# One weight load of a fused attention and mixture-of-experts kernel, issued by ScalarE instead of the sync engine

## The chip, the core and the metric

The kernel runs on one core of one Trainium2 chip. The metric is the device time of one execution in microseconds (us). Before the change it is 284.03 us, the median of three runs that lie between 283.61 and 284.60 us.

The core has five engines with an instruction stream each: PE (TensorE, matrix products), DVE (VectorE), ACT (ScalarE), POOL (GpSimd) and SP (SyncE, which here only issues transfers). PEld is PE's loading of weights. Sixteen DMA engines move data between HBM and the core's memory. A transfer is issued by an instruction on an engine's stream and goes into that engine's queue: q1 in the profile is SP's queue, q10 is ScalarE's.

## The reference

An attention with a decaying state runs over 768 steps for each of 4 batches and 8 heads of width 48; its output, 3072 rows of 384, goes through a mixture of 4 experts with weights of 384 x 1024 and 1024 x 384.

```
for t in range(S):
    cur = einsum('bhd,bhe->bhde', u * k[t], v[t])
    y[t] = einsum('bhd,bhde->bhe', r[t], state + cur)
    state = w * state + einsum('bhd,bhe->bhde', k[t], v[t])
x = y, laid out as (B*S) x (H*D)
p = domain_probs / (domain_probs.sum(-1) + 1e-9)
for e in range(E):
    out += p[:, e] * (relu(x @ w1[e]) @ w2[e])
```

## The kernel before, in words

The attention is done in 24 chunks of 128 rows; chunk ci belongs to batch ci modulo 4, so the first four chunks are the first of the four batches. For a chunk the kernel loads r, k and v (tiles `RKin` and `Vt`, 192 KB each, line 270), multiplies r and k by powers of w into `RK_sb` (line 429), transposes them on PE (line 498) and copies them out to `RKT` (lines 79 and 81), multiplies them to `At_all` (line 546), masks that into `AtM` on DVE (line 560), and multiplies by v to `Y_ps` (line 593). Beside it POOL forms r*k into `ruk` (line 446) and times u (line 454; line 451 on DVE for chunk 0), DVE sums it into `dcoef` (line 467) and POOL makes `dv` from it (line 472). The result is transposed to `xTe` (line 645). Groups of four chunks then go through the experts: the first layer is `hT_ps` (line 751, 757), its relu is on ACT (line 766, 768), the second layer is `out_ps` (line 787). Later groups use a scheme with sums and differences of halves (`M_ps`, line 966).

The weights come as float32 in three pieces for each expert and layer, `PIECES = ((0, 3), (3, 6), (6, 8))` in blocks of 128 columns: 576, 576 and 384 KB. They land in one of four staging slots of the tile `stg` and are cast to bf16 into `w_sb` (line 79 on ACT, 81 on DVE, 83 on POOL). The middle piece of w1 of expert 0 is `("wst", 1, 0, 1)`; its cast is the first of ACT's casts of weights.

The order of every engine's instructions is written out by hand: `PLAN` is a string that names each job and its engine, and the kernel emits the jobs in that order. `load_w` makes one load job; its `run` takes the first slot from `st_free`, and the cast gives it back. SP's stream begins with k of chunk 0, v of 1, r of 1, r of 0, k of 1, r of 2, v of 0, r of 3, k of 2, k of 3, and then the middle piece and the last piece of w1 of expert 0, v of 2, the first piece, and v of 3. ACT's stream begins with a table load and three small loads of w and u (lines 93, 95 and 102) before its first job, the logarithm of w (line 345), from which PE makes `w_ps` (line 349) and ACT the powers `W_ps` (line 358).

Transfers take eight semaphores (`DMAHW0` to `DMAHW7`) in turn, in program order and over both queues. A transfer is issued only when the one that had its semaphore before, eight transfers earlier, has landed.

`spin` (line 246) puts matrix products on PE that nobody reads: seven before the first real one, and a written number before some jobs.

Of the kernel before, what the change touches and what calls it, by code (L numbers as in the profile page):

```python
# [18 lines left out]
def kernel(  # L19
# [12 lines left out]
    nc = tc.nc  # L32
# [9 lines left out]
    Dm = moe_w1.shape[1]  # L42
    F = moe_w1.shape[2]
    NDB = Dm // 128
# [19 lines left out]
    NST = 4  # L64
    NSTG = 8
    stg = weights.tile([128, NSTG, 3 * Dm], F32)
    stg_f = stg.rearrange("p a b -> p (a b)")
    stg_b = stg_f.bitcast(BF16)
    early = hAll.rearrange("p a s c -> p (a s c)").bitcast(F32)[:, 3 * NFB * SUB * 64:]
    w1_v = moe_w1.rearrange("e (db p) f -> e p db f", p=128)  # L70
# [3 lines left out]
    PIECES = ((0, 3), (3, 6), (6, 8))  # L74
# [162 lines left out]
    tl = {}  # L237
# [14 lines left out]
    def load_job(name, nbytes_us, run, takes=(), needs=()):  # L252
        q_rank[0] += 1
        job(name, {"S": 0.5}, run, needs, q_rank[0], takes, (), nbytes_us)
# [17 lines left out]

    at_of = {}
    touched = set()
    st_free = list(range(NST))

    def st_at(i):
        return 3072 + i * 3 * Dm

    def load_w(m, e, i):  # L280
        a, bb = PIECES[i]

        def run():
            tl["wst", m, e, i] = st_free.pop(0)
            t = stg_f[:, st_at(tl["wst", m, e, i]):][:, 0:(bb - a) * Dm]
            if m == 1:
                nc.sync.dma_start(t.rearrange("p (d f) -> p d f", d=NDB),
                                  w1_v[e][:, :, a * 128:bb * 128])
            else:
                nc.sync.dma_start(t.rearrange("p (f d) -> p f d", d=Dm),  # L290
                                  w2_v[e][:, a:bb, :])
        nd = 24 if m == 1 else 8 * (bb - a)
        us = 0.555 * (bb - a)
        if (m, e) not in touched:
            us += 0.37 if touched else 0.68
            touched.add((m, e))
        load_job(("wst", m, e, i), (us, nd), run,
                 (("wst", m, e, i),))
# [24 lines left out]
    def cast(m, e, i, rank):  # L323
        a, bb = PIECES[i]
        n = bb - a

        def run(eng):
            st_free.append(tl["wst", m, e, i])
            t = stg_f[:, st_at(tl["wst", m, e, i]):][:, 0:3 * Dm]
            if m == 1:  # L330
                copy_on(eng, w1_sb[:, e, :, a * 128:bb * 128],
                        t[:, 0:n * Dm].rearrange("p (d f) -> p d f", d=NDB))
            else:
                copy_on(eng, w2_sb[:, e, a:bb, :].rearrange("p f d -> p (f d)"), t[:, 0:n * Dm])
        on = {"A": 0.36 * n, "V": (0.43 if m == 1 else 0.23) * n}
        if e == 0:
            on = {"A": 0.36 * n}
            if m == 2:
                on["P"] = 0.36 * n
        job(("cast", m, e, i), on, run, [("wst", m, e, i)], rank, (),  # L340
            (("wst", m, e, i),))
# [995 lines left out]
```

## Time and profile before

| | |
|---|---|
| time, median of three runs | 284.03 us |
| time of the profiled execution | 283.63 us |
| its span, first to last instruction | 281.8 us |
| PE busy | 274.6 us (97%) |
| DVE, ACT, POOL busy | 189.1, 183.5, 111.1 us |
| granted clock of TensorE, mean | 1.000 of full speed |
| moved by DMA | 43.22 MB |

The profiled execution has 1.83 us outside its span. A row of a timeline gives the start of a group of instructions in us from the span's start, its length, engine, line, operation, tiles written and read, count, and in brackets how long the engine stood idle before it and what ended that. For a DMA issue (SPq, ACTq) the length is that of the issuing instruction, not of the transfer. Rows of the stages give busy us of each engine, the granted clock, the share of the 16 DMA engines in use (packets can overlap, so it can pass 1) and GB/s.

### The profile page before, as it was taken

How to read it: one execution, taken by the hardware profiler on the slowest of the kernel's cores; microseconds unless marked ns; L12 is line 12 of the kernel's file. 1: busy time of each engine (PE TensorE's matmuls, PEld its weight loads, DVE VectorE, ACT ScalarE, POOL GpSimd, SP SyncE). 2: the span in 40 equal slices, each digit the busy share in tenths (PEclk: the TensorE clock that was granted, in tenths of full speed). 3: DMA queues.
4: the chain of work that ended last, by engine and by line, in shares of the span. 5: the costliest groups of instructions: out<-in, count | busy, mean ns of one | idle time of the engine just before them, and what ended most of it. 6: DMA issues, size and time to landing. Idle time of an engine off the chain costs nothing.

```text
span 281.8 us, 6864 instructions
## 1 busy us (share of the span) xinstructions
PE 274.6 (97%) x2741; PEld 197.1 (70%) x2762; DVE 189.1 (67%) x334; ACT 183.5 (65%) x348; POOL 111.1 (39%) x134
## 2 busy tenths in 40 slices
PE   7899999999999999999999999999999999999995
PEld 2568567676665445899445899445899544899895
DVE  5964878998779646777537787355888706776071
ACT  5586756798852889744788752789754788521840
POOL 1985243875566565326862406476012000000000
PEclk9999999999999999999999999999999999999999
DMA  7999999899998897585994376993775500110202
GB/s 150 240 320 330 282 230 270 224 228 284 269 198 171 162 192 191 88 173 110 203 184 97 88 111 122 169 254 22 151 124 96 140 28 2 32 26 2 84 2 84
DMA packets 133491, 43.22 MB, mean 153 GB/s; under 512 B 121658, under 2 KB 133436, under 8 KB 133460
## 3 DMA queue, kind: packets, MB, share of 16 engines
q1 hardware_dynamic: 133300, 42.74, 70.1%
q8 instruction: 21, 0.34, 0.5%
q14 instruction: 10, 0.08, 0.1%
q10 hardware_dynamic: 160, 0.05, 0.1%
HBM read 26.79 MB, written 4.72 MB: 112 GB/s over the span
## 4 chain that ended last, share of the span: by engine, by line
PE 93%; DVE 2%; DMA 1%; ACT 1%; issue 1%; SPq 1%; POOL 0%; POOLq 0%
PE hT_ps L757 34%; PE M_ps L966 28%; PE out_ps L787 7%; PE hT_ps L1174 4%; PE hT_ps L1208 4%; PE out_ps L1191 4%; PE hT_ps L751 2%; PE At_all L546 2%; PE Y_ps L593 2%; DMA RKin<-in_r_dram 1%; PE St_ps L662 1%; PE Y_ps L586 1%; PE At_all L1123 1%; PE M_two L1123 1%; PE spin_ps L246 1%; DVE AtM L560 1%
## 5 line engine op out<-in xcount | busy, mean ns | idle before, releaser
L768 ACT ACTIVATE hAll<-hT_ps 128x512 bf16<-128x512 f32 x152 | 86.4, 597 | 25.4 <-PE hT_ps L757 22.7
L757 PE MATMUL hT_ps<-stg,w_sb 128*128 128x512 bf16 x370 | 85.6, 379 | 0.6
L757 PEld LDWEIGHTS <-w_sb 128*128 128x128 bf16 x456 | 42.5, 98 | 45.6
L966 PEld LDWEIGHTS <-hAll 128*128 128x128 bf16 x800 | 65.7, 98 | 1.1
L622 ACT ACTIVATE stg<-dv,p_nat 128x384 bf16<-128x384 f32 x72 | 41.3, 611 | 10.6 <-DMA stg<-stg 5.3
L446 POOL TENSOR_TENSOR ruk<-RKin 128x384 f32<-128x384 f32 x24 | 26.6, 1114 | 29.5 <-DMA RKin<-in_r_dram 17.9
L472 POOL TENSOR_TENSOR dv<-Vt,dcoef 128x384 f32<-128x384 f32 x24 | 21.5, 898 | 40.8 <-DVE dcoef L467 27.4
L966 PE MATMUL M_ps<-w_sb,hAll 128*128 128x192 bf16 x400 | 36.9, 246 | 0.0
L1000 ACT COPY o_sb<-M_ps 128x192 f32<-128x192 f32 x35 | 10.9, 316 | 38.2 <-PE M_ps L966 37.9
L681 POOL TENSOR_TENSOR S<-Tn,wC 64x192 bf16<-64x192 f32 x32 | 22.8, 712 | 23.9 <-DVE Tn L671 21.5
L928 DVE TENSOR_TENSOR stg<-hAll 128x1024 bf16<-128x1024 bf16 (+1 forms) x15 | 12.5, 836 | 25.5 <-ACT hAll L768 15.4
L454 POOL TENSOR_TENSOR ruk<-ruk,U_sd 128x384 f32<-128x384 f32 x23 | 24.7, 1076 | 1.0
L928 DVE TENSOR_TENSOR hAll<-hAll 128x1024 bf16<-128x1024 bf16 (+1 forms) x30 | 23.8, 803 | 0.6 <-PE M_ps L966 0.5
L787 PE MATMUL out_ps<-w_sb,hAll 128*128 128x384 bf16 x128 | 22.8, 326 | 0.0
L966 PE MATMUL M_ps<-o_sb,hAll 128*128 128x192 bf16 x200 | 20.3, 246 | 0.0
L966 PE MATMUL M_ps<-w_mix,hAll 128*128 128x192 bf16 x200 | 20.1, 246 | 0.0
L434 DVE TENSOR_TENSOR RK_sb<-RKin,W_both 128x768 bf16<-128x768 f32 x16 | 18.3, 1141 | 1.8 <-DMA RKin<-in_k_dram 1.8
L757 PE MATMUL hT_ps<-xTe,w_sb 128*128 128x512 bf16 x65 | 17.8, 379 | 0.4
L787 PEld LDWEIGHTS <-hAll 128*128 128x128 bf16 x128 | 12.0, 98 | 7.4
L608 DVE TENSOR_TENSOR dv<-Y_ps,dv 128x384 f32<-128x384 f32 x18 | 9.9, 551 | 8.3 <-PE Y_ps L593 6.9
L563 DVE TENSOR_TENSOR AtM<-At_all,mask 128x1024 bf16<-128x1024 f32 x8 | 9.8, 1219 | 8.4 <-PE At_all L546 7.9
L1002 DVE TENSOR_TENSOR o_sb<-o_sb,M_ps 128x192 f32<-128x192 f32 x25 | 8.5, 350 | 9.6 <-PE M_ps L966 3.3
(123 smaller groups left out, 392.8 us busy)
## 6 DMA issues: line engine op xcount, KB each, us to landing
stg<-in_moe_w_dram SPq DMA_DIRECT2D x16, 576.0 KB, 7.1
RKin<-in_k_dram SPq DMA_DIRECT2D x24, 192.0 KB, 4.0
Vt<-in_v_dram SPq DMA_DIRECT2D x24, 192.0 KB, 3.5
RKin<-in_r_dram SPq DMA_DIRECT2D x24, 192.0 KB, 4.2
out_dram<-o_sb SPq DMA_DIRECT2D x23, 192.0 KB, 2.3
stg<-in_moe_w_dram SPq DMA_DIRECT2D x8, 384.0 KB, 5.8
stg<-stg SPq DMA_TRANSPOSE x36, 2.8
RKT<-RK_sb SPq DMA_TRANSPOSE x16, 3.9
```

The lines of the kernel that those rows point to most:

```text
L434: job(("scale", ci, 0), {"V": SCALE_US}, lambda: nc.vector.tensor_mul(RK[:, :, :, 0:D], tl["in", ci], W_both), [("Rt", ci), ("Kt", ci), (" ...
L446: nc.gpsimd.tensor_mul(tl["ruk", ci], tl["Rt", ci], tl["Kt", ci])
L454: nc.gpsimd.tensor_mul(tl["ruk", ci], tl["ruk", ci], U_sd)
L472: nc.gpsimd.tensor_mul(tl["dv", ci], tl["Vt", ci], tl["dcoef", ci].to_broadcast((128, H, D)))
L622: nc.scalar.mul(o, tl["Ysb", ci], p_nat[:, e, n_p:n_p + 1])
L681: nc.gpsimd.tensor_mul(S_new[pr, :, cl], Tn2[pr, tn_at[ci], :, cl], wC[pr, :, None].to_broadcast((P2, NP, D)))
L757: nc.tensor.matmul(ps[:, 0:n, :].rearrange("p a b -> p (a b)"), w1_sb[:, e, db, fb * 128:(fb + 1) * 128], xTe[:, x0 + db, s0:s0 + n, :].re ...
L768: nc.scalar.activation(hTs[:, fb, s0:s0 + n, :], ps[:, 0:n, :], AF.Relu)
L787: nc.tensor.matmul(ps, relu_tile(e, sc)[:, fb, s, :], w2_sb[:, e, fb, :], start=(fb == 0), stop=(fb == NFB - 1))
L928: nc.vector.tensor_tensor(o, x, y, op=op)
L966: nc.tensor.matmul(tl["P", sc, q, m], st, moving(m, hf, (n + 4) % 8), start=(opens and n == 0), stop=(hf == 1 and n == 7), skip_group_chec ...
L1174: nc.tensor.matmul(ps[:, f, :], w1_sb[:, e, db, (a + f) * 128:(a + f + 1) * 128], get_xTe(1)[:, db, s, :], start=(f == 0 and db == 0), sto ...
```

## The change

The middle piece of w1 of expert 0 gets the fourth staging slot for itself. Its load is issued on ScalarE's queue in the preamble, right behind the three small loads and ahead of the logarithm, and waits for nothing. Its place in SP's stream, behind k of chunk 3, is empty now. The free list begins with three slots; the cast gives the fourth back to it as before.

```
-    st_free = list(range(NST))
+    st_free = list(range(NST - 1))

     def st_at(i):
         return 3072 + i * 3 * Dm

+    nc.scalar.dma_start(stg_f[:, st_at(NST - 1):][:, 0:3 * Dm].rearrange("p (d f) -> p d f", d=NDB),
+                        w1_v[0][:, :, PIECES[1][0] * 128:PIECES[1][1] * 128])
+
     def load_w(m, e, i):
         a, bb = PIECES[i]

         def run():
-            tl["wst", m, e, i] = st_free.pop(0)
+            tl["wst", m, e, i] = NST - 1 if (m, e, i) == (1, 0, 1) else st_free.pop(0)
             t = stg_f[:, st_at(tl["wst", m, e, i]):][:, 0:(bb - a) * Dm]
+            if (m, e, i) == (1, 0, 1):
+                return
             if m == 1:
                 nc.sync.dma_start(t.rearrange("p (d f) -> p d f", d=NDB),
                                   w1_v[e][:, :, a * 128:bb * 128])
```

On ACT the start of the stream was this (`hAll` holds the rows of w and u at this time):

```order
L93 DMA hAll_72<-in_w_dram 1x384 [waits DVE_49]
L95 DMA hAll_72<-in_u_dram 1x384 [waits DVE_49]
L102 DMA hAll_72<-in_w_dram 4x2x48 [waits DVE_49]
L345 ACTIVATE hAll_72<-hAll_72 1x384 [waits DMAHW2_49]
L79 CAST Vb_149<-Vt_135 128x384 [waits DMAHW1_49]
```

and it is now this:

```order
L93 DMA hAll_72<-in_w_dram 1x384 [waits DVE_49]
L95 DMA hAll_72<-in_u_dram 1x384 [waits DVE_49]
L102 DMA hAll_72<-in_w_dram 4x2x48 [waits DVE_49]
L280 DMA stg_73<-in_moe_w1_dram 128x3x384
L350 ACTIVATE hAll_72<-hAll_72 1x384 [waits DMAHW2_49]
L79 CAST Vb_150<-Vt_136 128x384 [waits DMAHW1_49]
```

One load is added ahead of the logarithm; every later instruction keeps its place, and lines behind the change are five higher.

On SP the stream from the fourth load on was this (`RKin_133`, `137`, `147` and `162` hold r and k of chunks 0 to 3, `Vt_135`, `151` and `226` v of chunks 1, 0 and 2):

```order
L270 DMA RKin_133<-in_r_dram 128x8x48
L270 DMA RKin_137<-in_k_dram 128x8x48
L270 DMA RKin_147<-in_r_dram 128x8x48 [waits DMAHW0_49]
L270 DMA Vt_151<-in_v_dram 128x8x48 [waits DMAHW1_49]
L270 DMA RKin_162<-in_r_dram 128x8x48 [waits DMAHW2_49]
L270 DMA RKin_147<-in_k_dram 128x8x48 [waits DMAHW3_49]
L270 DMA RKin_162<-in_k_dram 128x8x48 [waits DMAHW4_49]
L287 DMA stg_73<-in_moe_w1_dram 128x3x384 [waits DMAHW5_49]
L287 DMA stg_73<-in_moe_w1_dram 128x3x256 [waits DMAHW6_49]
L270 DMA Vt_226<-in_v_dram 128x8x48 [waits DMAHW7_49]
```

and it is now this (the numbers of these tiles are one higher, up to `163`):

```order
L270 DMA RKin_134<-in_r_dram 128x8x48
L270 DMA RKin_138<-in_k_dram 128x8x48 [waits DMAHW0_49]
L270 DMA RKin_148<-in_r_dram 128x8x48 [waits DMAHW1_49]
L270 DMA Vt_152<-in_v_dram 128x8x48 [waits DMAHW2_49]
L270 DMA RKin_163<-in_r_dram 128x8x48 [waits DMAHW3_49]
L270 DMA RKin_148<-in_k_dram 128x8x48 [waits DMAHW4_49]
L270 DMA RKin_163<-in_k_dram 128x8x48 [waits DMAHW5_49]
L292 DMA stg_73<-in_moe_w1_dram 128x3x256 [waits DMAHW6_49]
L270 DMA Vt_226<-in_v_dram 128x8x48 [waits DMAHW7_49]
```

The 576 KB load is gone from the row behind k of chunk 3. The new load on ACT takes a semaphore early, so that each SP transfer from k of chunk 1 to k of chunk 3 waits for the one that stood a place later in the old turn: k of chunk 1 now waits for k of chunk 0 to land, r of chunk 2 for v of chunk 1, and the load of 384 KB waits for the moved load itself. PE's, DVE's and POOL's streams hold the same instructions in the same order.

## Rows read from the trace of the kernel before

**Rows 1.** Parts of the page: busy time of PE; shares of the chain by engine.
```profile
PE 274.6 (97%) x2741; PEld 197.1 (70%) x2762; DVE 189.1 (67%) x334; ACT 183.5 (65%) x348; POOL 111.1 (39%) x134
...
PE 93%; DVE 2%; DMA 1%; ACT 1%; issue 1%; SPq 1%; POOL 0%; POOLq 0%
```

**Rows 2.** Two stages of the span: busy time of each engine, clock, DMA.
```profile
0.00:17.00 17.00, 13.99 (x114) 6.95 (x115) 11.70 (x34) 10.63 (x20) 11.03 (x20) 1.00 0.91 218
17.00:250.00 233.00, 231.90 (x2295) 162.72 (x2312) 163.68 (x265) 161.50 (x305) 100.11 (x115) 1.00 0.77 164
```

**Rows 3.** Chain of waits up to 18 us: start, us, what.
```profile
2.65 4.20 DMA RKin<-in_r_dram
...
6.99 1.01 POOL ruk L446
...
8.03 0.55 DVE ruk L451
...
17.15 0.84 PE hT_ps L751 x15
```

**Rows 4.** Timeline of DVE and POOL around the first chunk.
```profile
6.21 0.55 DVE L429 TENSOR_TENSOR RK_sb<-RKin,W_ps 128x384 bf16<-128x384 f32 x1 [2.39 <-ACT W_ps L358]
6.94 1.02 DVE L429 TENSOR_TENSOR RK_sb<-RKin,W_ps 128x384 bf16<-128x384 f32 x2 [0.18 <-DMA RKin<-in_r_dram]
...
8.83 0.55 DVE L429 TENSOR_TENSOR RK_sb<-RKin,W_ps 128x384 bf16<-128x384 f32 x1
...
6.99 1.96 POOL L446 TENSOR_TENSOR ruk<-RKin 128x384 f32<-128x384 f32 x2 [5.26 <-DMA RKin<-in_r_dram]
```

**Rows 5.** Timeline of SP's issues, first 17 us.
```profile
0.73 0.44 SPq L270 DMA_DIRECT2D RKin<-in_k_dram  x1
...
3.40 0.89 SPq L270 DMA_DIRECT2D RKin<-in_k_dram  x1
4.34 1.43 SPq L270 DMA_DIRECT2D RKin<-in_r_dram  x1
...
9.16 1.57 SPq L287 DMA_DIRECT2D stg<-in_moe_w_dram  x2
```

**Rows 6.** Stages of the first 14 us, columns as in rows 2.
```profile
1.00:2.00 1.00, 0.95 (x3) 0.40 (x4) 0.95 (x4) 1.00 (x1) 0.73 (x4) 1.00 0.05 11
2.00:11.00 9.00, 7.82 (x43) 3.26 (x41) 6.32 (x22) 4.90 (x11) 3.93 (x5) 1.00 1.08 213
6.00:7.00 1.00, 0.52 (x6) 0.18 (x4) 0.61 (x2) 1.00 (x3) 0.01 (x1) 1.00 0.85 162
7.00:14.00 7.00, 6.28 (x72) 3.56 (x70) 6.84 (x14) 4.21 (x10) 6.92 (x8) 1.00 0.99 238
11.00:12.00 1.00, 0.92 (x17) 0.73 (x17) 0.99 (x4) 0.07 (x1) 1.00 (x2) 1.00 0.49 97
12.00:14.00 2.00, 1.76 (x24) 1.19 (x24) 1.91 (x4) 1.66 (x4) 2.00 (x3) 1.00 0.98 343
```

**Rows 7.** Timeline of ACT: its issues, the logarithm, two casts.
```profile
2.27 0.75 ACTq L102 DMA_DIRECT2D hAll<-in_w_dram  x1
3.62 0.52 ACT L345 ACTIVATE hAll<-hAll 1x384 f32<-1x384 f32 x1 [1.61 <-DMA hAll<-in_w_dram]
4.42 0.51 ACT L79 CAST Vb<-Vt 128x384 bf16<-128x384 f32 x1 [0.27 <-DMA Vt<-in_v_dram]
...
14.87 1.15 ACT L79 CAST w_sb<-stg 128x1152 bf16<-128x1152 f32 x1
```

**Rows 8.** DMA queues, first 12 us: packets, MB, time as share of 16 engines.
```profile
q1 hardware_dynamic: 10435, 2.02, 85.1%
q10 hardware_dynamic: 16, 0.00, 0.2%
```

**Rows 9.** Timeline of PE at the first transposes.
```profile
7.05 0.92 PE L246 MATMUL spin_ps<-hAll 128*128 128x512 bf16 x4
7.82 0.39 PE L498 MATMUL RKT_ps<-ident,RK_sb 128*128 128x128 bf16 x4
```

## The prediction

> **What bounds the kernel now.** I read the page first, then two stages, then the chain of waits at the start. PE is busy 274.6 us of 281.8 and holds 93% of the chain [rows 1]. The stages say where it is not busy: it works 231.90 of the 233.00 us between 17 and 250 us, but only 13.99 of the first 17.00 [rows 2]. So from 17 us on PE is the bound, at full granted clock, and a delay of its start moves the end one for one; nothing later can give it back, since hardly a microsecond of idle time lies in those 233 us. In the first 17 us the chain does not run through PE alone [rows 3]: it leaves a DMA, the load of r of chunk 0, issued at 2.65 and 4.20 us under way, so landed at 6.85. From there it goes to POOL (`ruk`, 6.99), DVE (`ruk` times u, 8.03), and in the end to the expert's first layer at 17.15. DVE shows the same: at 6.94 it had waited 0.18 us for that load, and POOL, which had nothing to do before, took up both its products then [rows 4]. The reader is to see that what the change touches is this stretch, where transfers set the pace, and that the weight itself is not what is waited for: its cast stands at 14.87 with no idle time before it [rows 7].
>
> **The engines that move data are full then.** Between 2 and 11 us the share in use is 1.08, at 213 GB/s; between 12 and 14, where the weights move, it is 0.98 at 343 GB/s [rows 6]. All of it is SP's queue: ScalarE's moved 16 packets in the first 12 us [rows 8]. One input of 192 KB (196.6 thousand bytes) takes 0.92 us at 213 GB/s, and the ten that stand ahead of the weights 9.2 us. From 2.0 us, about where data begin to move (11 GB/s in the second before), they fill the time to 11.2, and the row at 11 to 12 us shows the gap that follows, share 0.49 [rows 6]. By this count r of chunk 0, fourth in SP's stream, has the engines from 4.8 to 5.7 us; it is landed 1.2 us later.
>
> **The change part by part.**
>
> *The issue on ACT.* It stands behind the third small load, which begins at 2.27 and takes 0.75, so it begins at 3.02 [rows 7]. SP's two issues of weights took 1.57 us together, 0.79 each [rows 5]. It ends at 3.8, where the logarithm began at 3.62: 0.2 us late, with the powers of w and DVE's first product behind it (6.21 to 6.76, then 6.94, [rows 4]). 0.18 of it lies under DVE's wait for r; and when r comes later, all of it does. I count nothing. If the issue takes as long as SP's longest of inputs, 1.43 [rows 5], the logarithm is 0.8 late and the product of chunk 0 some 0.6 if r is on time: this end is kept for the range.
>
> *The issue taken from SP.* 0.79 us of SP's time go, behind k of chunk 3. What comes earlier is the last piece of w1, v of 2 and on. None of them is waited for by PE's work in the first 17 us. Nothing gained.
>
> *The semaphores.* k of chunk 1, issued at 3.40, now waits for k of chunk 0 to land. That had happened by 4.34, since r of chunk 2 waited for the same and began then [rows 5]; so at most 0.94 us. r of chunk 2 waits for v of chunk 1, which was there at 4.42 (ACT's cast of it begins, [rows 7]). Both slips stay inside the backlog: k of chunk 1 would not have its turn before 5.7, and in the next step not before 7. The 384 KB load waits for the moved one, issued six us ahead of it. Nothing, with up to 0.9 kept for the upper end.
>
> *The transfer.* This is the term. 589.8 thousand bytes at 343 GB/s are 1.72 us of all sixteen engines. They used to be spent behind the ten inputs and are now spent among them. An issue led to the first data 1.2 us after its start (k of chunk 0: 0.73, data at 2.0, [rows 5, 6]), so the moved load has data from 4.2 on, when SP's queue still has 1.5 us of work up to the end of r of chunk 0. The trace has no stretch in which both queues carry anything of size, so I bound it from both sides. Below: the weights fit in what the small rows leave unused, 343 less 213 = 130 GB/s; r is on time, cost 0, and not below, for no transfer ahead of r is removed. Above: all 1.72 us go ahead of the end of r. Between them, if the engines give each queue half of their time, 1.5 us of r and its predecessor cost 1.5 us; if the data begin 0.6 us later, because the issue takes longer beside SP's, 0.9 us are left to share and cost 0.9. A share of 1.08 is nearest to the rows of full engines, so I take a value among the last three, 1.4. The loads behind r are late by about as much, less 0.24 us that the thin row at 6 to 7 us (162 for 213 GB/s) can take up; they were used just when they were due (the product of chunk 2 at 8.83, POOL's second one directly behind the first, [rows 4]), so even where r alone came on time, they would hold POOL and DVE by more than a microsecond.
>
> The Trainium skill weighs in on the side of the cost. "DMA: Bandwidth & Descriptors", section "Issuing engines are not separate DMA queues", says that transfers started by several engines end on the same sixteen DMA engines and interleave, so that a second issuing engine saves only issue time. Its section "Queues, rings and completion order" has each engine take turns between queues by whole packets of some 9 to 17 descriptors. Each DMA engine has 24 rows of this weight to move, 384 over 16; by that rule two or three turns carry them all, and the sum would be the upper 1.72. That ScalarE's queue is apart from SP's the trace agrees with [rows 8]; how they share, no run here shows yet.
>
> *Does anything absorb it?* Hardly: from 7 to 14 us POOL is busy 6.92 and DVE 6.84 of 7.00 us [rows 6], and PE's idle time there is made by them. PE's extra products before the transposes are there at 7.05 to 7.97, and the transposes at 7.82 follow them [rows 9]: they would now end before r is in, and PE would stand still for a little over a microsecond. PE loses what r loses.
>
> **The sum.** On the profiled execution, 283.63 = 281.8 of span and 1.83 around it: 283.63 + 1.4 = 285.0. That execution lies 0.40 below the median of the three runs, 284.03; on the median the forecast is 285.4 us, 0.5% slower.
>
> **The rivals.**
>
> *No slower: the weights fit beside the inputs.* For it: the inputs move at 213 GB/s and weights at 343, so bytes are not what fills the engines, and 589.8 thousand bytes at 130 GB/s take 4.5 us, from 4.2 to 8.7, six before the cast. Against it: the share of 1.08 says that the small packets fill the engines' time. It decides if the lateness of r stays below 0.4. Time 284.0 to 284.4; I put it at 284.1, chance 0.2.
>
> *Slower by more.* r is late by the full 1.72, and something is added: k of chunk 1 late by its new wait, the logarithm behind a long issue, or the granted clock of PE, 1.00 in every stage (2.4 GHz), falling to the lower level when PE stands idle and the extra products are spent ahead of the gap. The extra products and first small products up to 12 us would run at 1.2 GHz; 0.92 us of them cost as much again. 1.72 + 0.9 = 2.6: 286.6, up to 287.2. For it: PE's gap gets longer than any in these rows save the start. Against it: that start, 1.05 us of idle time, was followed by the full clock. Chance 0.14.
>
> *Faster.* The gap at 11 to 12 us is filled, 0.5 us, and all weights behind it come earlier, SP being freed too. For it: POOL's casts do wait on weights later. Against it: PE has no idle time there. It pays only if r itself lands sooner, and then at most DVE's 0.18 before its next input. With what the measurement adds, 283.1 at best; chance 0.06.
>
> **How the numbers follow.** Forecast case 0.60, with its own range 284.9 to 286.0. A difference under 0.3%, 0.85 us, is about what can't be told from no change here. Slower by more: 0.60 + 0.14 = 0.74; within: 0.20; faster: 0.06. The range goes from 283.8, which takes in the case of no cost and half of the runs' spread below the median, to 287.2, the top of the worse case.
>
> **What would show it.** After the change the chain of waits still leaves r of chunk 0, landed at 8.2 and not 6.85; POOL's first `ruk` begins near 8.4; DVE's wait for r is 1.3 to 1.6 and not 0.18; ScalarE's queue has 0.59 MB early on; the first stretch of the DMA engines runs at more GB/s, the gap at 11 to 12 is gone; the expert's first layer begins near 18.5 and everything behind is shifted by the same. It would be wrong if `ruk` began before 7.4 (the weights fit), if r were late and the first layer of the expert were not (a slack that I missed), or if the granted clock fell below 1.00.

## The result, and the profile after

The changed kernel takes 287.22 us (median of 286.82, 285.64, 287.73 and 287.61), against 284.04 for the kernel before in the same series: a ratio of 1.0108, with an interval of 1.0082 to 1.0133. The sign and the path of the loss were forecast; the size was not. The forecast was 285.4 in a range from 283.8 to 287.2: the median lies at the very top of it, and the loss, 3.2 us, is more than twice the 1.4 that was forecast. The profiled execution is the one of 286.82: its span is 285.0 us where it was 281.8, so 3.2 us are to be found.

Two parts of the page after, busy time of the engines and granted clock of PE in 40 slices, answer to [rows 1]:

```profile
PE 276.7 (97%) x2741; PEld 197.9 (69%) x2762; DVE 189.4 (66%) x334; ACT 183.1 (64%) x348; POOL 110.7 (39%) x134
...
PEclk9799999999999999999999999999999999999999
```

PE executes the same 2741 instructions, yet is busy 2.1 us longer, and the second slice of 7.1 us shows why: the granted clock is no longer full there. The stages say where the time went (busy time of each engine, clock, DMA share, GB/s, as in [rows 2]):

```profile
0.00:17.00 17.00, 13.39 (x80) 6.22 (x81) 10.23 (x31) 7.77 (x15) 8.67 (x17) 0.90 0.89 205
20.00:250.00 230.00, 228.89 (x2246) 159.69 (x2265) 161.93 (x261) 160.42 (x303) 99.56 (x115) 1.00 0.77 162
```

Between 20 and 250 us PE works 228.89 us; before, it worked 228.90 in the same stretch:

```profile
20.00:250.00 230.00, 228.90 (x2239) 160.16 (x2258) 160.68 (x260) 158.94 (x301) 97.94 (x112) 1.00 0.77 163
```

PE has as little idle time there as before, so all 3.2 us arise before about 20 us. In the first 17 us only 80 matmul instructions ran instead of 114, at a clock of 0.90. The chain of waits of that beginning (start, us, what) answers to [rows 3]:

```profile
2.69 6.47 DMA RKin<-in_r_dram
...
9.25 0.57 DVE RK_sb L434
...
9.86 0.41 PE RKT_ps L503 x4
...
12.42 2.01 PE spin_ps L246 x6
```

The load of r of chunk 0 is under way for 6.47 us instead of 4.20 and lands at 9.15 instead of 6.85: 2.30 us late. Behind it everything slips, as the timelines of DVE, POOL and PE show (start, us, then in brackets the idle time before and what ended it); the first three rows answer to [rows 4], the next to [rows 9], the last to the layer at 17.15 in [rows 3]:

```profile
6.42 0.55 DVE L434 TENSOR_TENSOR RK_sb<-RKin,W_ps 128x384 bf16<-128x384 f32 x1 [2.60 <-ACT W_ps L363]
9.25 1.02 DVE L434 TENSOR_TENSOR RK_sb<-RKin,W_ps 128x384 bf16<-128x384 f32 x2 [2.27 <-DMA RKin<-in_r_dram]
...
9.30 1.95 POOL L451 TENSOR_TENSOR ruk<-RKin 128x384 f32<-128x384 f32 x2 [7.56 <-DMA RKin<-in_k_dram]
...
9.86 0.40 PE L503 MATMUL RKT_ps<-ident,RK_sb 128*128 128x128 bf16 x4 [1.67 <-DVE RK_sb L434]
...
12.21 2.22 PE L246 MATMUL spin_ps<-hAll 128*128 128x512 bf16 x6
...
20.18 1.00 PE L756 MATMUL hT_ps<-xTe,w_sb 128*128 128x128 bf16 x15
```

DVE waits 2.27 us for r where it waited 0.18. POOL is released 2.31 later; the name of its releaser, k, is only the last by the profile. PE stands idle for 1.67 us, and the expert's first layer begins its fifteen matmuls at 20.18. Before, the layer and the six extra products stood here:

```profile
9.53 1.46 PE L246 MATMUL spin_ps<-hAll 128*128 128x512 bf16 x6
...
16.99 1.00 PE L751 MATMUL hT_ps<-xTe,w_sb 128*128 128x128 bf16 x15
```

The layer is 3.19 later, nearly 0.9 more than r is late. This rest is the clock:

```profile
10.00:11.00 1.00, 0.92 (x6) 0.19 (x4) 0.94 (x3) 0.71 (x2) 1.00 (x2) 0.66 1.08 198
11.00:12.00 1.00, 0.73 (x10) 0.53 (x11) 1.00 (x3) 0.73 (x2) 0.92 (x2) 0.50 0.87 158
12.00:13.00 1.00, 1.00 (x6) 0.52 (x5) 1.00 (x3) 0.54 (x2) 1.00 (x2) 0.50 1.05 209
13.00:14.00 1.00, 1.00 (x4) 0.40 (x3) 0.88 (x2) 0.42 (x2) 1.00 (x2) 0.63 1.13 216
```

PE works again from 9.86 on, and then the clock falls: the two rows from 11 to 13 us are at 0.50, the level of 1.2 GHz, those before and behind them at 0.66 and 0.63, and from 14 us on the clock is full again. The six extra products in the row of 12.21 take 2.22 us; the same six took 1.46 before, so these alone cost 0.76.

The stages of half a microsecond around the moved load show what happens to the DMA engines:

```profile
4.00:4.50 0.50, 0.35 (x1) 0.35 (x2) 0.00 (x0) 0.10 (x1) 0.00 (x0) 1.00 1.21 244
4.50:5.00 0.50, 0.50 (x2) 0.20 (x2) 0.00 (x0) 0.46 (x1) 0.00 (x0) 1.00 0.79 140
5.00:5.50 0.50, 0.50 (x2) 0.10 (x1) 0.00 (x0) 0.05 (x1) 0.00 (x0) 1.00 0.66 166
5.50:6.00 0.50, 0.50 (x3) 0.41 (x2) 0.00 (x0) 0.17 (x1) 0.00 (x0) 1.00 0.89 284
6.00:7.00 1.00, 1.00 (x2) 0.14 (x1) 0.55 (x1) 0.86 (x2) 0.00 (x0) 1.00 1.08 348
```

The weight drives the rate to 348 GB/s, as the weights did between 12 and 14 us before [rows 6]. But from 4.5 to 6 us the share in use is 0.79, 0.66 and 0.89, where the mean of the stretch before the change was 1.08. Against that mean these three rows leave 0.5 × (0.29 + 0.42 + 0.19) = 0.45 us of the engines unused, while r waits in SP's queue. The rows from 7 to 8.5 us, not printed here, stand above the mean (1.15, 1.24 and 1.26), so that over all of 4 to 9 us the share is 1.02.

### The profile page after: what moved, and what is told of

Its sections match the earlier page's. It is cut to its first block, busy times and chain, and to the rows that moved or that the text cites. A ratio compares the mean times of both kernels' runs of the same rounds, so it can differ in the third digit from the quotient of the medians.

```text
span 285.0 us, 6864 instructions
## 1 busy us (share of the span) xinstructions
PE 276.7 (97%) x2741; PEld 197.9 (69%) x2762; DVE 189.4 (66%) x334; ACT 183.1 (64%) x348; POOL 110.7 (39%) x134
## 4 chain that ended last, share of the span: by engine, by line
PE 93%; DMA 2%; ACT 1%; DVE 1%; SPq 1%; issue 1%; DVEq 0%
PE hT_ps L762 34%; PE M_ps L971 27%; PE out_ps L792 7%; PE hT_ps L1179 4%; PE hT_ps L1213 4%; PE out_ps L1196 4%; DMA RKin<-in_r_dram 2%; PE At_all L551 2%; PE hT_ps L756 2%; PE Y_ps L598 2%; PE spin_ps L246 1%; PE St_ps L667 1%; PE Y_ps L591 1%; PE RKT_ps L503 1%; PE At_all L1128 1%; PE M_two L1128 1%
## 5 line engine op out<-in xcount | busy, mean ns | idle before, releaser
L451 POOL TENSOR_TENSOR ruk<-RKin 128x384 f32<-128x384 f32 x24 | 25.6, 1075 | 32.6 <-DMA RKin<-in_r_dram 13.1
L439 DVE TENSOR_TENSOR RK_sb<-RKin,W_both 128x768 bf16<-128x768 f32 x16 | 19.0, 1188 | 1.7 <-DMA RKin<-in_k_dram 1.7
L565 DVE TENSOR_TENSOR AtM<-At_ps,mask 128x512 bf16<-128x512 f32 x16 | 10.7, 684 | 6.4 <-PE At_ps L551 6.2
```

Of the source, the lines that this page charges most:

```text
L439: job(("scale", ci, 0), {"V": SCALE_US}, lambda: nc.vector.tensor_mul(RK[:, :, :, 0:D], tl["in", ci], W_both), [("Rt", ci), ("Kt", ci), (" ...
L451: nc.gpsimd.tensor_mul(tl["ruk", ci], tl["Rt", ci], tl["Kt", ci])
```

## The experiments

Each was run beside the kernel before on the same chip. The theory to be tested is that the bytes of the weight go ahead of r of chunk 0; its rivals are the shifted semaphores, the issue on ScalarE, the second queue, and the clock.

### The load moves; the queue stays ScalarE's (late)

The load is issued where load_w runs, behind ScalarE's first copy of powers, at 8.19 us; r has landed by then.

```
-    nc.scalar.dma_start(...)            # the preamble's issue is gone
     if (m, e, i) == (1, 0, 1):
+        nc.scalar.dma_start(t.rearrange("p (d f) -> p d f", d=NDB), w1_v[e][:, :, a * 128:bb * 128])
         return
```

> The load stays on ScalarE's queue but is issued where SP issued it before, behind ACT's first copy of the powers of w (about 9.2 us). Theory A (the early weight takes the DMA engines from r of chunk 0): r lands at 6.85 again, 284.0 +- 0.4. Theory B (the price is in ScalarE's queue itself, its semaphore turn or the issue on ACT): still slower by 1 us or more, 285 to 287.

Measured: 286.07 us, ratio 1.0065 [1.0041, 1.0089]. The expected return to the time before did not come, and by the numbers alone theory B would fit. DVE's and PE's timelines and one stage:

```profile
6.15 1.64 DVE L434 TENSOR_TENSOR RK_sb<-RKin,W_ps 128x384 bf16<-128x384 f32 x3 [2.33 <-ACT W_ps L363]
...
14.62 0.40 PE L503 MATMUL At_all<-ident,RK_sb 128*128 128x128 bf16 x4 [1.19 <-POOL RK_sb L434]
...
16.00:17.00 1.00, 1.00 (x6) 0.38 (x4) 0.42 (x1) 1.00 (x3) 1.00 (x2) 0.50 1.11 345
```

r of chunk 0 is on time: DVE goes through its three products without a break. But the weight now goes ahead of the inputs of chunks 2 and 3, still in SP's queue: the chain of waits leads back to a load of k that was 6.08 us under way from 7.43 on. PE waits 1.19 us for the product that POOL makes from it, and the clock falls to 0.50 afterwards. It is the same kind of loss, on a later chunk; that it is not ScalarE's queue itself is shown by `behind`, below.

### The semaphore turns alone (tiny)

The kernel before, with 1.5 KB loaded by ScalarE in the same place. This shifts the semaphore turns of SP's loads up to k of chunk 3 as the change does, and moves next to nothing. (Behind k of chunk 3 the turns differ, since SP's load of the weight still takes one.)

```
+    nc.scalar.dma_start(stg_f[0:1, st_at(NST - 1):][:, 0:384], w1_v[0][0:1, 0, 384:768])
```

> The kernel before, with one more load of 1.5 KB on ScalarE's queue in the place where the change issues 576 KB; the weight itself stays in SP's stream. It shifts the turn of the semaphores as the change does, but moves no bytes to speak of. Theory A (bytes): 284.0 +- 0.4, r of chunk 0 lands at 6.9. Theory C (the new waits of SP's loads for semaphores are the price): k of chunk 1 is issued at 3.6 and the loads behind it late, 285 or more.

Measured: 284.03 against 283.92, ratio 1.0001 [0.9983, 1.0020]. k of chunk 1 is issued at 3.69, as late as in the change (3.61). The new waits and a small issue cost nothing that can be told, to within 0.2%.

### A third of the bytes (third)

One of the three blocks (192 KB) goes early on ScalarE's queue, the other two on SP's in the old place.

```
-    nc.scalar.dma_start(stg_f[...][:, 0:3 * Dm]..., w1_v[0][:, :, PIECES[1][0] * 128:PIECES[1][1] * 128])
+    nc.scalar.dma_start(stg_f[...][:, 0:Dm]..., w1_v[0][:, 0:1, PIECES[1][0] * 128:PIECES[1][1] * 128])
     if (m, e, i) == (1, 0, 1):
+        nc.sync.dma_start(t.rearrange(...)[:, 1:], w1_v[e][:, 1:, a * 128:bb * 128])
```

> Only one of the three blocks of the piece, 192 KB in 128 rows of 1536 bytes, is loaded early on ScalarE's queue; the other 384 KB stay in SP's stream. Theory A, by bytes: r of chunk 0 is late by a third of 1.75 to 2.3 us, 0.6 to 0.8, and the time 284.6 to 284.9, with PE's clock at 1.00. Theory D (a second queue in use costs a fixed time, whatever the bytes): r late by over 1.5 us, 285.6 or more.

Measured: 284.71 us, ratio 1.0021 [1.0006, 1.0036]. DVE's timeline:

```profile
7.63 1.02 DVE L436 TENSOR_TENSOR RK_sb<-RKin,W_ps 128x384 bf16<-128x384 f32 x2 [1.08 <-DMA RKin<-in_r_dram]
```

r's product begins 0.69 later than at 6.94 [rows 4]; a third of 2.30 would be 0.77, a third of 1.72 is 0.57. The lateness goes with the bytes. PE keeps its full clock (mean 1.000), and the expert's first layer is 0.70 late (17.69), by what r is.

### More extra products in front of the gap (spins)

The change, with the extra products ahead of the first transposes raised to fill PE's pause and hold the clock.

```
-    SPINS = {..., ('T', 0, 0): 10, ...
+    SPINS = {..., ('T', 0, 0): 34, ...
```

> The changed kernel with 24 quarters, six more products of 128x512, on PE ahead of the second transpose of chunk 0, where PE stood idle 1.67 us for r; nothing else is changed. If part of the 3.2 us is PE's clock (0.50 from 11 to 13 us after that idle time): granted clock 1.00 in all runs, r still lands near 9.15, and the time is 285.7 to 286.1. If the clock is only a sign and costs nothing: no gain, 286.8 to 287.6, or a loss by the added products.

Measured: 287.1 us, ratio 1.0107 [1.0086, 1.0128]. PE's timeline:

```profile
6.66 1.89 PE L246 MATMUL spin_ps<-hAll 128*128 128x512 bf16 x8
10.77 0.27 PE L246 MATMUL spin_ps<-hAll 128*128 128x128 bf16 x2 [2.22 <-DVE ruk L456]
```

The last products had to wait for a buffer that DVE frees only after r, so that the pause became 2.22 us instead of 1.67. As a test of whether a shorter pause holds the clock it says nothing; `spins2` is that test. But it prices the clock: three of its six executions, at a mean clock of 0.994, took 287.64 us on the mean, the three at 0.999 and above 286.53, 1.1 us less.

### Behind all inputs (behind)

The load on ScalarE's queue, issued behind its second copy of powers, at 9.96 us.

```
+            if j.name == ("Wsb", 0):
+                nc.scalar.dma_start(stg_f[:, st_at(NST - 1):][:, 0:3 * Dm]..., w1_v[0][...])
```

> The load is again issued on ScalarE, but behind ACT's second copy of the powers of w, at about 10.3 us, so that its data begin when the inputs of chunks 2 and 3 have been moved (11.2 us). The run that issued it at 8.2 us was 2.1 us slower though r of chunk 0 was on time: PE waited 1.19 us for POOL's product of chunk 3. Theory A, widened (the weight on its own queue overtakes whatever inputs SP's queue still holds): with nothing left to overtake, 284.0 +- 0.4 and no such wait. Theory B (ScalarE's queue or the issue on ACT costs by itself): 285 to 286.5 again.

Measured: 284.26 against 283.48, ratio 1.0023 [1.0007, 1.0038]. ACT's and PE's timelines:

```profile
16.14 1.15 ACT L79 CAST w_sb<-stg 128x1152 bf16<-128x1152 f32 x1 [1.41 <-DMA stg<-in_moe_w_dram]
17.41 0.36 PE L596 MATMUL Y_ps<-Vb,AtM 128*128 128x48 bf16 x8 [0.57 <-ACT wC L380]
```

The inputs are on time, and most of the loss is gone: ScalarE's queue as such does not cost microseconds. What stays is a cast that waits 1.41 us for the weight, and 0.57 us of PE behind ScalarE. So of the places tried on ScalarE's queue none is free: earlier the load delays inputs, here it is late itself.

### The old queue, the early place (sp_early)

The kernel before, with the load put in SP's queue right ahead of r of chunk 0.

```
+    w_at = [n for n, (j, e) in enumerate(plan) if j.name == ("wst", 1, 0, 1)][0]
+    w_item = plan.pop(w_at)
+    plan.insert([n for n, (j, e) in enumerate(plan) if j.name == ("Rt", 0)][0], w_item)
```

> The kernel before, with the same load in SP's queue but moved up to stand right ahead of r of chunk 0; ScalarE's queue is as before. If the price is the engines' time spent on the weight ahead of the inputs: r is late by 1.7 us at least, lands at 8.5 to 8.8, and the time is 285.7 to 286.2 with the clock at 1.00, about 287 where it falls. If a second queue is what hurts: r late by 0.8 at most (SP's longer issue), 284.0 to 284.9.

Measured: 286.27 us, ratio 1.0094 [1.0067, 1.0122]. DVE's timeline and two stages:

```profile
9.22 1.02 DVE L429 TENSOR_TENSOR RK_sb<-RKin,W_ps 128x384 bf16<-128x384 f32 x2 [2.25 <-DMA RKin<-in_r_dram]
...
4.50:5.00 0.50, 0.50 (x2) 0.20 (x2) 0.00 (x0) 0.32 (x1) 0.00 (x0) 1.00 0.73 137
5.00:5.50 0.50, 0.50 (x2) 0.10 (x1) 0.00 (x0) 0.20 (x1) 0.00 (x0) 1.00 0.34 115
```

With one queue DVE waits 2.25 us, with two 2.27. The price is the order of the bytes, not the second queue, and ScalarE's issue has no part in it. r lands at 9.1, later than the 8.5 to 8.8 that were expected: here too it is late by more than the 1.72 us of the bytes. The thin stretch at the weight's start is here too, thinner still. Two of the four executions kept the full clock; they took 285.77 us on the mean, the two at 0.994 took 286.80.

The Trainium skill's "DMA: Bandwidth & Descriptors", section "Issuing engines are not separate DMA queues", says that a second issuing engine saves only issue time, since all transfers end on the same engines. These two runs agree: 2.25 and 2.27 us.

### The clock held (spins2)

The change, with nine extra products in two buffers that are free, so that PE's pause is shorter.

```
+                if j.name == ("T", 0, 0):
+                    spin(2); spin(7)
+                else:
                     spin(SPINS[j.name] // 4)
                     spin(SPINS[j.name] % 4, 1)
```

> As the run with more products on PE ahead of the second transpose of chunk 0, but nine of 128x512 in all, in two buffers that are free, since there two of them waited 2.2 us for a buffer and PE stood idle longer than without them. If PE's idle time is what lowers the clock: granted clock 1.00 in nearly all executions, and a time of 285.7 to 286.2, near the execution of the changed kernel that kept its clock (285.64). If not: 286.8 to 287.6 as the changed kernel.

Measured: 285.83 us, ratio 1.0076 [1.0056, 1.0096], with the clock at 0.998 or above in each execution. PE's timeline, DVE's, and a stage:

```profile
9.87 0.40 PE L503 MATMUL RKT_ps<-ident,RK_sb 128*128 128x128 bf16 x4 [0.95 <-DVE RK_sb L434]
...
9.26 1.02 DVE L434 TENSOR_TENSOR RK_sb<-RKin,W_ps 128x384 bf16<-128x384 f32 x2 [2.95 <-DMA RKin<-in_r_dram]
...
19.31 1.00 PE L756 MATMUL hT_ps<-xTe,w_sb 128*128 128x128 bf16 x15
...
11.00:12.00 1.00, 1.00 (x14) 0.47 (x14) 1.00 (x3) 0.75 (x2) 0.92 (x2) 1.00 1.01 196
```

r is as late as in the change (9.26 against 9.25), PE's pause is 0.95, and the clock stays at 1.00 where it was 0.50. With the full clock the first layer is late by just what r is, 2.32 us, and the span is 284.2, 2.4 above before. In ratios, 0.32% of 283.5 us came back, 0.9 us, though the intervals of the two ratios overlap. The executions within each run bear the size out: in sp_early, measured beside spins2, those that kept the clock took 285.77 us on the mean, as spins2's four did, and those that lost it 1.0 more; in spins it is 1.1, in late 1.3. The change's own are wider apart, one at 1.000 with 285.64 and three at 0.993 to 0.994 with a mean of 287.39. So the clock costs about 0.9 us where it falls.

That a pause of this length makes it fall is not shown. In dup_large, below, PE stood still longer and kept the full clock through the whole profiled execution:

```profile
9.99 0.40 PE L501 MATMUL RKT_ps<-ident,RK_sb 128*128 128x128 bf16 x4 [1.81 <-DVE RK_sb L432]
```

Its first layer then began at 19.43, 2.44 late, and r's product was 2.44 late.

### Extra bytes with long rows, and with short ones (dup_large, dup_small)

In both the real load stays in SP's old place, and 576 KB that nobody reads are loaded early on ScalarE's queue: once the weight's rows of 1536 bytes, once rows of r of 192 bytes.

```
+    nc.scalar.dma_start(stg_f[:, st_at(NST - 1):][:, 0:3 * Dm]..., w1_v[0][...])                     # dup_large
+    nc.scalar.dma_start(stg_f[...].rearrange("p (n f) -> p n f", f=48), r.rearrange(...)[0:C, 0:24, :])  # dup_small
```

> The kernel before, with one more transfer that nobody reads: the 576 KB of the weight piece, in rows of 1536 bytes, on ScalarE's queue where the change has them; SP loads the piece again where it did. It is the control for the next run. Theory A: r of chunk 0 lands at 9.0 to 9.2, as after the change, and the weight's packets hold 0.6 to 0.9 of the engines between 5.5 and 7 us.

> The same as the control, but the 576 KB are read from r in rows of 192 bytes, the size of the inputs' rows: 3072 packets instead of 384. Theory A1 (the engines take turns packet by packet, so a big packet takes more of the time): both queues get about half, the 0.4 to 0.8 us that r of chunk 0 still needed cost as much again, and r lands at 7.3 to 7.9, though all packets of the added transfer together hold the engines 2.9 us. Theory A2 (the added transfer goes ahead as a whole): r lands at 9.5 or later.

Measured: dup_large 286.62 us, ratio 1.0047 [1.0016, 1.0078], from a series in which the kernel before itself scattered from 283.67 to 286.39; dup_small 286.69, ratio 1.0076 [1.0047, 1.0105]. DVE's timeline of the two, large first:

```profile
9.38 1.02 DVE L432 TENSOR_TENSOR RK_sb<-RKin,W_ps 128x384 bf16<-128x384 f32 x2 [2.41 <-DMA RKin<-in_r_dram]
```

```profile
9.13 1.02 DVE L432 TENSOR_TENSOR RK_sb<-RKin,W_ps 128x384 bf16<-128x384 f32 x2 [2.71 <-DMA RKin<-in_r_dram]
```

In dup_large r is as late with SP's load still in its place (it lands at 9.28, just above the 9.0 to 9.2 expected), and the loss is no larger than the change's: nothing shows that freeing SP of the load gave anything back. dup_small missed both expectations: neither the 7.3 to 7.9 of turns by packet, nor 9.5 and more of a queue that goes first. What the queues did (packets, MB, share of 16 engines), from 5.5 to 7 us in the change, then in dup_small:

```profile
q10 hardware_dynamic: 272, 0.41, 76.0%
q1 hardware_dynamic: 403, 0.08, 25.6%
```

```profile
q10 hardware_dynamic: 1449, 0.28, 95.1%
q1 hardware_dynamic: 391, 0.08, 24.4%
```

In the change the two counts are of one size, but ScalarE's packets are eight times as long, so the weight takes five of six bytes and r is put off by nearly all of it. In dup_small the packets are equally long and yet the counts are 1449 to 391. Part of that may be that r was issued later: SP's third and fourth issue took 2.33 us there, 1.51 before, and between 5.5 and 6 us SP's queue moved nothing at all. From 7 to 8 us, where both queues moved throughout, each moved 679 packets, which fits turns by packet. Why SP's queue stood still before that stays open.

The Trainium skill's "DMA: Bandwidth & Descriptors", section "Queues, rings and completion order", has each engine alternate between queues by packets of several descriptors. The change's counts, 272 and 403, would go with it, and so would dup_small's 679 and 679 from 7 to 8 us; its 1449 and 391 from 5.5 to 7 do not show such turns, and decide nothing more.

## Why the prediction was right in kind and wrong in size

*What bounds the kernel: right.* From 20 to 250 us PE works 228.89 us after and 228.90 before; the end moves with the start: the first layer is 3.19 later, the span 3.2 longer.

*The issue on ACT: right.* It took 0.46 us, not 0.79, and the logarithm began at 3.57, where it had begun at 3.62 [rows 7].

*The issue taken from SP: right.* dup_large keeps it, has r as late, and loses no more.

*The semaphores: right, by tiny.* The changed kernel issues k of chunk 1 at 3.61 instead of 3.40, inside the backlog.

*The transfer: this step failed.* It was put at 1.4 us within 0 to 1.72, and measured 2.30. Its first mistake is the choice: in sp_early, where all of the weight is ahead of r, r is no later than in the change, so the whole 1.72 had to be taken. The argument of half the time for each queue gave r too much: from 5.5 to 7 us r's queue got one of six bytes. Its second mistake is that 1.72 was called an upper bound. The size itself was right: ScalarE's packets took 13.7% of the engines' first 12 us, 1.64 us. But r was late by 0.58 more, and what makes up the 0.58 stays open. Two things that the sum left out can be read in the traces, and neither fits all runs. The first is that a weight piece does not begin at the full rate of rows 6: 0.45 us of the engines went unused from 4.5 to 6 us, 0.60 in sp_early. But in spins2 these three rows are 1.30, 0.67 and 0.99, and r is as late. The second is that loads behind r got ahead of its last packets: when r landed, SP's queue had moved 1.02 MB before and 1.14 MB after the change, and 0.12 MB at 213 GB/s are an estimated 0.6 us. But in sp_early, as late, it had moved 1.60 MB with the weight's 0.59 in it, so no more inputs than before. The trace of before held the first of these: the gap that I read as the end of the inputs at 11 to 12 us [rows 6] stands where the first weight begins. In stages of half a microsecond, of the kernel before:

```profile
11.00:11.50 0.50, 0.41 (x12) 0.45 (x13) 0.49 (x2) 0.00 (x0) 0.50 (x1) 1.00 0.55 117
11.50:12.00 0.50, 0.50 (x12) 0.27 (x8) 0.49 (x2) 0.07 (x1) 0.50 (x2) 1.00 0.43 77
12.00:12.50 0.50, 0.49 (x10) 0.28 (x10) 0.41 (x2) 0.50 (x2) 0.50 (x1) 1.00 0.87 280
```

Against 1.08 that is 0.70 us unused. In the change the thin stretch stands at the moved weight's start, in front of r. Two runs have an early transfer on ScalarE's queue without it: third, with one block instead of three (its share is 1.06, 1.08 and 1.15 from 4.5 to 6 us), and dup_small, with short rows (1.11, 1.20 and 1.14). In dup_small r is 2.19 late all the same. What makes the gap was not settled.

*The loads behind r: right.* r of chunk 0 alone on time does not help, as late shows.

*Does anything absorb it? Right that nothing does; the clock makes it worse.* The rival "slower by more" named the pause, the extra products spent ahead of it, and a price of 0.9 us on top of the full 1.72. It is the rival that came true: the clock fell in three of four executions, and spins2 measures 0.9. I gave the falling clock too little chance because the pause of 1.05 us at the start had been followed by the full clock; one of 1.67 us was not. The clock did not fall each time, though (sp_early lost it in two of four executions, dup_large in two of eight), so that a chance was the right form for it; 0.14 was low.

*The rival that the weights fit: wrong.* r would have had to be late by less than 0.4 us and was by 2.30; the 130 GB/s left beside short rows were not there. *The rival of a faster kernel: wrong;* PE had no time to give back.

Of the signs named, r landed at 9.15 (8.2 was said), `ruk` began at 9.30 (8.4), DVE waited 2.27 us (1.3 to 1.6), and the expert's layer began about 3.2 late (1.35). ScalarE's queue moved its 0.59 MB in the first 12 us, the stretch from 4 to 9 us ran at 257 GB/s where it had run at 210, and the gap at 11 to 12 us was gone, with a share of 0.87. The clock fell below 1.00, which was named as what would make the forecast wrong. With the measured sizes in place of 1.4, the sum is 283.63 + 2.30 + 0.9 = 286.8; the profiled execution took 286.82.

No version tried beats the kernel before: the nearest are tiny, which is that kernel but for 1.5 KB, third, 0.21% slower, and behind, 0.23% slower.

## What to carry to other kernels

Here a load that was issued early on an idle queue was not free, because the transfer engines were full: it went ahead of what was still waiting in the other queue. These loads feed the chain of waits, so their lateness reached the end in full: the whole time of the bytes, 1.72 us, and 0.58 more. Before moving a load, count what it will be in front of, and take the time of its bytes as the likely price rather than as the worst; read a thin row in the DMA share as a possible start of a transfer, not only as room. When a delay opens a pause on PE ahead of dense work, price the lower clock with a chance as part of the forecast, since here it was 0.9 of 3.2 us in three of four executions.

## What the runs showed that was not expected

- A 576 KB weight piece with rows of 1536 bytes behind inputs of short rows left the engines thinly used for one to one and a half microseconds: 0.45 us unused in the change, 0.70 in the kernel before, 0.60 in sp_early; a 192 KB piece of the same rows did not. The lateness of r did not follow it.
- A pause of 1.67 us of PE at 8 to 10 us was followed by the clock at 0.50 between 11 and 13 us, in late one of 1.19 us by 0.50 at 16 to 17 us; in spins2 pauses of 0.95 and 0.67 left it at 1.00, and in dup_large so did one of 1.81.
- While ScalarE's queue moved short rows, SP's queue moved no packet for half a microsecond; from 7 to 8 us the two moved 679 packets each.
